# A weight conversion on four engines without its VectorE maximum: the scale of an activation keeps the shifted-out bits at zero

## The chip, the cores and the metric

The kernel runs on one core of a Trainium2 chip. The metric is the device time of one execution in microseconds (us). The kernel before takes 1225.82 us, the median of 3 runs between 1224.88 and 1225.98. One further execution was recorded by the hardware profiler, and every duration and wait that is quoted below comes from that one.

## The reference

The reference is an attention with random features, followed by a mixer over tokens and channels. The four weight tensors U, V, w_ch1 and w_ch2 of the mixer arrive as 64-bit floats, since `np.sqrt` makes them so; everything else is float32.

```python
# attention: batch 8, heads 8, sequence 576, head_dim 64, features 128
proj = x @ w_phi
proj = proj - max(abs(proj), axis=-1)
phi(x) = concat([exp(proj), exp(-proj)], axis=-1)
kv = sum over s of phi(k)[s,f] * v[s,d];  z = sum over s of phi(k)[s,f]
attn = (phi(q) @ kv) / (phi(q) @ z + 1e-6)
# mixer: x = attn as [8, 576, 512], U 576x32, V 32x576, w_ch1 512x2048, w_ch2 2048x512
u = x + (x^T @ U @ V)^T
out = u + max(u @ w_ch1, 0) @ w_ch2
```

## The kernel before

TensorE (PE) does all matrix products. A float32 operand that needs its full precision is split into a high and a low part, and three products (high by high, high by low, low by high) are summed. The hidden layer of the mixer is cut into 16 blocks f of 128 columns: `hidden` (line 619) makes one block of 512 tokens, and `add` (line 640) brings it through the second weight into the four output banks. One mixer pass g handles 512 tokens; there are nine of them. The attention of pairs of heads (`Pair`) runs in between, in steps such as `s_project_k0`, `s_kv1` or `s_out0`, and the class `Pace` hands out chunks of the mixer between the steps so that PE always has something to do.

The weights are loaded once, as 64-bit words, and converted on the chip. That is the function `convert` (line 130), called once for U, twice for V and 32 times for the blocks of w_ch1 and w_ch2 (two for each f). Each 64-bit float is turned into float32 like this. ScalarE (ACT) makes three pieces with three activations: two 16-bit pieces of the lower part (lines 137 and 138), and the size of the upper word, which is the absolute value of that word read as a float32, scaled by a power of two (line 140). VectorE (DVE) brings that size to a least value (line 141) and shifts its bits left by three (line 142), so that the 11-bit exponent of the 64-bit format becomes the 8-bit exponent of float32. GpSimd (POOL) adds the two halves as 64-bit integers (line 146). `split_w` then makes the two parts of the weight: a copy on ACT for w_ch1 or on DVE for w_ch2 (line 235), and a subtraction on DVE (line 236). In the names, `words` is the raw block, `w_ab` the scratch tile of the conversion, `w` the finished parts.

Only the first mixer pass (g = 0) needs blocks just converted; the conversions are spread over the time in which that pass and the attention of the first batches run (the constant `CONVERT`, and `blocks` in `mix`). On top of that, a scheduler sets the order of the instructions on each engine: it lays the whole program out with its own estimates of how long each instruction takes, so that leaving out one instruction can move others. Each engine then works through its list strictly in order. DVE, ACT and POOL are shared with the attention: line 348 and 350 (the maximum and the subtraction of the key features, `kp`), 364 (the subtraction of the query features, `qp`), 363 (the maximum over partitions on POOL for the query features), 625 (the low part of a hidden block, `h_lo`) and 319 (the low part of turned inputs, `T`) are the ones that matter below. PSUM banks are handed on in turn within a group: three banks carry the tag `at`, so a new tile there has to wait until the last reader of the tile that held its bank is done.

Of the kernel before, what the change touches and what calls it, by code (L numbers as in the profile page):

```python
# [16 lines left out]
AF = mybir.ActivationFunctionType  # L17
# [8 lines left out]
def tile_kernel(  # L26
# [12 lines left out]
    nc = tc.nc  # L39
# [33 lines left out]
    def f32(ap):  # L73
        return ap.bitcast(F32)
# [47 lines left out]
    def scratch(name, dt=F32, shape=(2, 512)):  # L122
        return moe.tile([P, *shape], dt, tag="wide", bufs=NW, name=name)
# [6 lines left out]
    def convert(st, name):  # L130

        n = st.shape[1]
        halves = st.rearrange("p n w -> p (n w)").bitcast(U16).rearrange("p (n h) -> p n h", h=4)
        ab = scratch(f"{name}_ab", I32)
        a, b_ = ab[:, 0, 0:n], ab[:, 1, 0:n]
        bh = b_.bitcast(U16).rearrange("p (n h) -> p n h", h=2)
        nc.scalar.activation(out=bh[:, :, 0], in_=halves[:, :, 1], func=AF.Copy, scale=2.0 ** -13)
        nc.scalar.activation(
            out=bh.bitcast(F16)[:, :, 1], in_=f32(st[:, :, 1]), func=AF.Copy, scale=2.0 ** -60)
        nc.scalar.activation(out=f32(a), in_=f32(st[:, :, 1]), func=AF.Abs, scale=2.0 ** -48)  # L140
        nc.vector.tensor_scalar_max(out=f32(a), in0=f32(a), scalar1=2.0 ** -63)
        nc.vector.tensor_scalar(  # L142
            out=a, in0=a, scalar1=3, scalar2=None, op0=ALU.logical_shift_left)

        a64, b64 = a.bitcast(U64), b_.bitcast(U64)
        nc.gpsimd.int64_add(a64, a64, b64)  # L146
        return f32(a)
# [3 lines left out]
    def load_uv():  # L151
        st = scratch("u_st", I32, (512, 2))[:, 0:(NT + 1) * R, :]
        sv = st.rearrange("p (t r) w -> p t r w", r=R)
        nc.sync.dma_start(
            out=sv[:, 0:NT], in_=U[0:SM].rearrange("(t p) r w -> p t r w", t=NT))
        for g in range(2):
            nc.sync.dma_start(out=sv[g * ST:(g + 1) * ST, NT], in_=U[SM:S])
        u_f = convert(st, "u").rearrange("p (t r) -> p t r", r=R)
        nc.vector.memset(f32(u_all[:, NT:NT + 2]), 0.0)
        parts = [(slice(0, P), slice(0, NT), slice(0, NT))]  # L160
        for g in range(2):
            parts.append((slice(g * ST, (g + 1) * ST), slice(NT + g, NT + g + 1), slice(NT, NT + 1)))
        for pr, to, of in parts:
            nc.vector.tensor_copy(out=u_all[pr, to, 0, :], in_=u_f[pr, of])
            nc.vector.tensor_sub(u_all[pr, to, 1, :], u_f[pr, of], f32(u_all[pr, to, 0, :]))
            for i in (2, 3):
                nc.vector.tensor_copy(out=u_all[pr, to, i, :], in_=f32(u_all[pr, to, 0, :]))

        for cs in (slice(0, SM), slice(SM, S)):
            n = cs.stop - cs.start  # L170
            st = scratch(f"v_st{cs.start}", I32, (512, 2))[:, 0:n, :]
            for g in range(4):
                nc.sync.dma_start(out=st[g * R:(g + 1) * R], in_=V[:, cs])
            v_f = convert(st, f"v{cs.start}")
            vm = v_all[:, cs]
            nc.vector.tensor_copy(out=vm, in_=v_f)
            lo = slice(3 * R, 4 * R)
            nc.vector.tensor_sub(vm[lo], v_f[lo], f32(vm[lo]))
# [36 lines left out]
    def convert_block(i):  # L215
        f, n = divmod(i, 2)
        r = convert(words[f][n], f"w{n + 1}_{f}")
        if f not in WHOLE:
            w = home.tile([P, 2, C], F32R, tag=f"w{n + 1}_{f}", name=f"w{n + 1}_{f}")
            split_w((nc.scalar.copy, nc.vector.tensor_copy)[n], r, w)  # L220
        elif n == 0:
            found[f] = r
            return
        else:
            w1_w, w = place(f, F32R, (2, C), f"w_{f}")
            split_w(nc.scalar.copy, found[f], w1_w)
            split_w(nc.vector.tensor_copy, r, w)
            w1_t[f] = w1_w
        (w1_t, w2_t)[n][f] = w
        if f in STREAM:  # L230
            for i in range(2) if f in WHOLE else (n,):
                nc.sync.dma_start(out=kept[f][:, i], in_=f32((w1_t, w2_t)[i][f]))
# [700 lines left out]
```

## Time and profile before

| what | value |
|---|---|
| median of 3 runs | 1225.82 us (1224.88 to 1225.98) |
| the profiled execution's own time | 1229.95 us |
| its span, first to last instruction | 1228.2 us |
| mean TensorE clock granted | 0.993 |
| busy: PE, DVE, ACT, POOL | 98%, 56%, 44%, 17% |
| line 141 on `w_ab` | 32 instructions, 20.3 us, 635 ns on average |
| first and last start of line 141 on `w_ab` | 47.3 us and 231.8 us |

A busy share is an average over the whole span. In the page's row of 40 slices a slice is about 31 us, and each digit is the busy share of that slice in tenths. "PEclk" is the clock that TensorE was granted, and 1.00 is full speed. The chain of waits goes back from the last instruction, at each step to what released it; a row of it gives the start, the time that this piece takes on the chain, the engine and the line. In a row of a group, the two figures behind the bar are the total busy time and the mean in ns of one instruction; consecutive instructions on DVE overlap a little, so a piece of the chain is shorter than the duration of its instruction.

### The profile page before, as it was taken

To read this page: it belongs to the slowest core of one execution; us is meant where nothing else is said; L and a number is where in the kernel's file an instruction comes from. 1 tells how busy PE (TensorE), PEld (TensorE's weight loads), DVE (VectorE), ACT (ScalarE), POOL (GpSimd) and SP (SyncE) were. 2 spreads that over 40 slices of the span, in tenths; PEclk is the share of its full clock that TensorE was granted. 3 is DMA by queue.
4 is the path that set the end of the run, shared out by engine and by line. 5 is a ranking of instruction groups with operands and counts; after the bars stand their busy time and mean duration, and the time that the engine had idled before them with its cause. 6 is when DMAs were issued, how large, how long until landed. Compare 5 with 4: busy or idle time off the path is not lost.

```text
span 1228.2 us, 18295 instructions
## 1 busy us (share of the span) xinstructions
PE 1204.1 (98%) x6667; PEld 1036.8 (84%) x6669; DVE 690.3 (56%) x1517; ACT 538.6 (44%) x1151; POOL 204.3 (17%) x154
## 2 busy tenths in 40 slices
PE   8999998999999999999999999999999999999998
PEld 7887887888888888888888888888888888888886
DVE  5858779775566656665556556755556543311211
ACT  6866678544443444444434444344534431111110
POOL 3533434211110111011111111011101110000000
PEclk9979999999999999999999999999999999999999
DMA  4766221341234213431244123431353014510201
GB/s 128 244 224 203 82 65 30 78 120 22 54 92 115 58 27 88 106 99 30 64 109 114 30 52 84 106 79 23 79 121 99 1 50 122 142 34 1 69 1 35
DMA packets 248409, 100.60 MB, mean 82 GB/s; under 512 B 215424, under 2 KB 227968, under 8 KB 248320
## 3 DMA queue, kind: packets, MB, share of 16 engines
q1 hardware_dynamic: 248000, 98.92, 31.0%
q8 instruction: 53, 0.87, 0.3%
q10 hardware_dynamic: 320, 0.52, 0.1%
q14 instruction: 36, 0.29, 0.1%
HBM read 78.41 MB, written 20.97 MB: 81 GB/s over the span
## 4 chain that ended last, share of the span: by engine, by line
PE 79%; DVE 7%; SPq 4%; ACT 4%; DMA 3%; issue 2%; POOL 0%; DVEq 0%; ACTq 0%; POOLq 0%
PE ph L619 27%; PE o L640 27%; PE xp L482 7%; PE kv_ps L443 7%; SPq L605 2%; PE pk L399 2%; DVE w L236 2%; SPq L265 1%; PE pp L561 1%; PE pq L422 1%; PE kv_ps L436 1%; PE pq L423 1%; DMA raw<-in_q_dram 1%; PE xpt L469 1%; DMA words<-in_moe_w_ch_dram 1%
## 5 line engine op out<-in xcount | busy, mean ns | idle before, releaser
L619 PE MATMUL ph<-uT_hi,w 128*128 128x512 f32 x1152 | 388.8, 395 | 4.2 <-DVE h_lo L625 2.9
L640 PE MATMUL o<-w,h_hi 128*128 128x512 f32 x1152 | 327.5, 395 | 3.0 <-ACT h_hi L624 3.0
L619 PEld LDWEIGHTS ph<-uT_hi,w 128*128 128x128 f32 x1152 | 216.2, 188 | 50.1 <-DVE h_lo L625 4.3
L640 PEld LDWEIGHTS o<-w,h_hi 128*128 128x128 f32 x1152 | 211.1, 188 | 45.1 <-ACT h_hi L624 4.7
L619 PE MATMUL ph<-uT_lo,w 128*128 128x512 f32 x576 | 225.1, 391 | 0.0
L624 ACT ACTIVATE h_hi<-ph 128x512 fp32r<-128x512 f32 x144 | 86.0, 597 | 268.2 <-PE ph L619 257.3
L625 DVE SCALAR_TENSOR_TENSOR h_lo<-ph,h_hi 128x512 fp32r<-128x512 f32 x144 | 98.6, 685 | 175.8 <-ACT h_hi L624 174.5
L640 PE MATMUL o<-w,h_lo 128*128 128x512 f32 x576 | 192.5, 395 | 0.4 <-DVE h_lo L625 0.4
L363 POOL PARTITION_ALL_REDUCE qp<-qp x64 | 127.3, 1989 | 288.2 <-ACT qp L362 269.7
L443 PEld LDWEIGHTS kv_ps<-vb,kp 128*128 128x128 f32 x1024 | 126.7, 195 | 2.8
L482 PEld LDWEIGHTS xp<-kv,qp 128*128 128x128 f32 x1024 | 124.0, 194 | 5.0 <-DVE kp L403 0.9
L619 PEld LDWEIGHTS ph<-uT_lo,w 128*128 128x128 f32 x576 | 108.3, 188 | 21.4 <-DVE uT_lo L244 0.6
L443 PE MATMUL kv_ps<-vb,kp 128*128 128x65 f32 x1024 | 126.1, 274 | 0.1
L482 PE MATMUL xp<-kv,qp 128*128 128x65 f32 x1024 | 124.1, 274 | 0.6 <-DVE kp L403 0.6
L640 PEld LDWEIGHTS o<-w,h_lo 128*128 128x128 f32 x576 | 105.4, 188 | 21.3 <-DVE h_lo L625 1.0
L353 ACT ACTIVATE kp<-kp 128x512 f32<-128x512 f32 x64 | 40.4, 631 | 134.4 <-DVE kp L350 79.4
L363 POOL PARTITION_ALL_REDUCE qp_t<-qp_t x32 | 27.3, 853 | 400.4 <-ACT qp_t L362 398.2
L319 DVE TENSOR_TENSOR T<-raw,T 64x512 fp32r<-64x512 f32 x96 | 67.6, 704 | 33.5 <-ACT T L318 31.0
L315 DVE STREAM_TRANSPOSE raw<-raw 128x512 f32<-128x512 f32 x48 | 34.1, 711 | 83.3 <-DMA raw<-in_q_dram 36.9
L318 ACT CAST T<-raw 64x512 fp32r<-64x512 f32 x96 | 59.3, 618 | 33.7 <-PE pq L423 18.2
L365 ACT ACTIVATE qp<-qp 128x512 f32<-128x512 f32 x64 | 40.4, 631 | 61.5 <-DVE qp L364 61.0
L146 POOL INT64_ADD w_ab<-w_ab x32 | 44.2, 1380 | 76.0 <-DVE w_ab L142 35.8
(128 smaller groups left out, 1357.7 us busy)
## 6 DMA issues: line engine op xcount, KB each, us to landing
words<-in_moe_w_ch_dram SPq DMA_DIRECT2D x32, 512.0 KB, 8.8
w<-kept SPq DMA_DIRECT2D x30, 512.0 KB, 4.0
vb<-in_v_dram SPq DMA_DIRECT2D x64, 128.0 KB, 2.5
u_dram<-x SPq DMA_DIRECT2D x32, 256.0 KB, 2.2
st<-u_dram SPq DMA_DIRECT2D x16, 512.0 KB, 3.9
out_dram<-st SPq DMA_DIRECT2D x32, 256.0 KB, 2.4
y<-u_dram SPq DMA_DIRECT2D x112, 64.0 KB, 2.4
raw<-in_k_dram SPq DMA_DIRECT2D x192, 32.0 KB, 2.0
```

Source lines behind the costliest of these rows:

```text
L146: nc.gpsimd.int64_add(a64, a64, b64)
L318: nc.scalar.copy(out=m[here, s, :], in_=x_[here])
L319: nc.vector.tensor_sub(m[there, s, :], x_[here], f32(m[here, s, :]))
L353: nc.scalar.activation(out=kp[:, :, 0:F], in_=kp[:, :, F:2 * F], func=AF.Exp)
L363: nc.gpsimd.partition_all_reduce(qp[:, 0, :], qp[:, 1, :], P, ReduceOp.absmax)
L365: nc.scalar.activation(out=qp[:, 0, :], in_=qp[:, 1, :], func=AF.Exp)
L443: nc.tensor.matmul(self.kv_v[:, f, g, :], kp[:, t, f * F:(f + 1) * F], self.vb[:, g, t, :], start=False, stop=(t == NT - 1), skip_group_ch ...
L482: nc.tensor.matmul(xv[:, c, :], qp[:, f, c * P:(c + 1) * P], self.kv[:, f, c // 2 if self.split else s, :], start=(f == 0), stop=(f == 1))
L619: nc.tensor.matmul(ph, w1_part(f, l, c), r[:, c, :], start=(n == 0), stop=(n == 3 * NCC - 1))
L624: on_act = nc.scalar.activation(out=h_hi, in_=ph, func=AF.Relu)
L625: on_dve = nc.vector.scalar_tensor_tensor(out=h_lo, in0=ph, scalar=0.0, in1=f32(h_hi), op0=ALU.max, op1=ALU.subtract)
L640: ins = nc.tensor.matmul(self.o[t], l[:, cs], w2_t[f][:, r, :], start=(f == 0 and n == 0), stop=(f == NFC - 1 and n == 2))
```

## The change

`convert` loses the maximum of line 141. The scale of the activation ahead of it goes from 2^-48 to 2^-112. Before, the scaled size still had the bit at the top of its exponent that the shift pushed out, and the maximum with 2^-63 made sure that this bit was always set. Now the exponent is so small that the bits which the shift pushes out are all zero. Below that, the shift and the integer addition are the same.

```diff
@@ convert
         nc.scalar.activation(
             out=bh.bitcast(F16)[:, :, 1], in_=f32(st[:, :, 1]), func=AF.Copy, scale=2.0 ** -60)
-        nc.scalar.activation(out=f32(a), in_=f32(st[:, :, 1]), func=AF.Abs, scale=2.0 ** -48)
-        nc.vector.tensor_scalar_max(out=f32(a), in0=f32(a), scalar1=2.0 ** -63)
+        nc.scalar.activation(out=f32(a), in_=f32(st[:, :, 1]), func=AF.Abs, scale=2.0 ** -112)
         nc.vector.tensor_scalar(
             out=a, in0=a, scalar1=3, scalar2=None, op0=ALU.logical_shift_left)
```

35 instructions leave DVE's list (32 of `w_ab`, two of V, one of U); no engine gets another one. The list of every engine is the same from about 270 us on; ahead of that, the scheduler has moved instructions. In the changed kernel the line numbers from 141 on are one lower: 141 is the shift there, 145 the integer addition, 234 and 235 the copy and the subtraction of a weight.

The first place is on DVE at about 54 to 60 us. `w_0` and `w_1` are the first two weight blocks (two conversions each), `pk_0_3` is the bank of projected keys that the last row frees. Before:

```order
L141 TENSOR_SCALAR w_1_ab<-w_1_ab 128x512
L461 TENSOR_TENSOR xt_267<-xpt_2_714,den_2_t_717 64x64
L456 TENSOR_SCALAR den_2_t_721<-xpt_2_714 64x1
L565 TENSOR_TENSOR pst_600<-pp_0_601,pst_600 32x256
L235 CAST w_0_928<-w_0_ab 128x512
L142 TENSOR_SCALAR w_1_ab<-w_1_ab 128x512
L141 TENSOR_SCALAR w_1_ab<-w_1_ab 128x512
L457 RECIPROCAL den_2_t_721<-den_2_t_721 64x1
L236 TENSOR_TENSOR w_0_891<-w_0_ab,w_0_891 128x512
L456 TENSOR_SCALAR den_2_0_734<-xp_0_2_725 128x4
L350 TENSOR_TENSOR kp_3_1_743<-pk_0_3_740,mk_3_1_744 128x4x128
```

And in the changed kernel:

```order
L347 TENSOR_REDUCE mk_3_1_741<-pk_0_3_737 128x4
L234 CAST w_0_923<-w_0_ab 128x512
L235 TENSOR_TENSOR w_0_887<-w_0_ab,w_0_887 128x512
L460 TENSOR_TENSOR xt_267<-xpt_2_711,den_2_t_714 64x64
L455 TENSOR_SCALAR den_2_t_718<-xpt_2_711 64x1
L141 TENSOR_SCALAR w_1_ab<-w_1_ab 128x512
L235 TENSOR_TENSOR w_0_923<-w_0_ab,w_0_923 128x512
L456 RECIPROCAL den_2_t_718<-den_2_t_718 64x1
L363 TENSOR_TENSOR qp_3_t<-qp_3_t 128x128
L455 TENSOR_SCALAR den_2_0_731<-xp_0_2_722 128x4
L349 TENSOR_TENSOR kp_3_1_740<-pk_0_3_737,mk_3_1_741 128x4x128
```

The second subtraction of `w_0`, the second shift of `w_1` and the subtraction of `qp_3_t` now stand ahead of the row that reads `pk_0_3` last; before, they came behind it.

The second place is on POOL at the same time (`ISA` on `w_ab` is the integer addition, on `qp` the maximum over partitions). Before:

```order
L146 ISA w_0_ab<-w_0_ab 128x512
L363 ISA qp_2_1_652<-qp_2_1_652 128x512
L309 MEMSET tail_T_0_787 128x256
L146 ISA w_0_ab<-w_0_ab 128x512
L363 ISA qp_3_t<-qp_3_t 128x128
L146 ISA w_1_ab<-w_1_ab 128x512 x2
```

And in the changed kernel:

```order
L145 ISA w_0_ab<-w_0_ab 128x512
L362 ISA qp_2_1_649<-qp_2_1_649 128x512
L145 ISA w_0_ab<-w_0_ab 128x512
L308 MEMSET tail_T_0_784 128x256
L145 ISA w_1_ab<-w_1_ab 128x512
L362 ISA qp_3_t<-qp_3_t 128x128
L145 ISA w_1_ab<-w_1_ab 128x512
```

The first addition of `w_1` now stands ahead of the maximum of `qp_3_t`.

The third place is on DVE at about 197 to 204 us, ahead of `h_lo_10`, the low part of a hidden block, for which PE waits. Before:

```order
L141 TENSOR_SCALAR w_13_ab<-w_13_ab 128x512
L297 TENSOR_TENSOR tail_T_0_2052<-tT_0_2050,tail_T_0_2052 64x2x64
L315 STREAM_TRANSPOSE raw_1_0_2160<-raw_1_0_2160 128x512
L142 TENSOR_SCALAR w_13_ab<-w_13_ab 128x512
L297 TENSOR_TENSOR tail_T_0_2052<-tT_0_2050,tail_T_0_2052 64x2x64
L319 TENSOR_TENSOR T_2_0_2063<-raw_0_1_1856,T_2_0_2063 64x512
L364 TENSOR_TENSOR qp_3_0_2017<-qp_3_0_2017 128x512
L319 TENSOR_TENSOR T_2_0_2063<-raw_0_1_1856,T_2_0_2063 64x512
L625 SCALAR_TENSOR_TENSOR h_lo_10_2135<-ph_10_2121,h_hi_10_2134 128x512
```

And in the changed kernel:

```order
L314 STREAM_TRANSPOSE raw_1_0_2130<-raw_1_0_2130 128x512
L141 TENSOR_SCALAR w_13_ab<-w_13_ab 128x512
L363 TENSOR_TENSOR qp_3_0_1990<-qp_3_0_1990 128x512
L296 TENSOR_TENSOR tail_T_0_2024<-tT_0_2022,tail_T_0_2024 64x2x64
L234 CAST w_12_2047<-w_12_ab 128x512
L318 TENSOR_TENSOR T_2_0_2035<-raw_0_1_1832,T_2_0_2035 64x512 x2
L235 TENSOR_TENSOR w_12_2047<-w_12_ab,w_12_2047 128x512
L296 TENSOR_TENSOR tail_T_0_2024<-tT_0_2022,tail_T_0_2024 64x2x64
L235 TENSOR_TENSOR w_13_2088<-w_13_ab,w_13_2088 128x512
L624 SCALAR_TENSOR_TENSOR h_lo_10_2105<-ph_10_2091,h_hi_10_2104 128x512
```

The first subtraction of `w_13` now stands ahead of `h_lo_10`; before, it came eight instructions behind it. (The copy and the subtraction of `w_12` came just ahead of the rows shown before.)

## The prediction

> **What bounds the kernel now.** I read the page first, then the stretches of time, then the chain of waits inside the stretch that counts.
>
> ```profile
> span 1228.2 us, 18295 instructions
> ...
> PE   8999998999999999999999999999999999999998
> PEld 7887887888888888888888888888888888888886
> DVE  5858779775566656665556556755556543311211
> ```
>
> PE is full nearly everywhere, and DVE is heavily loaded only in the first eight slices, up to about 250 us. The line that goes, 141, runs only there (47 to 232 us). Three stretches show what that means:
>
> ```profile
> 50.00:80.00 30.00, 28.37 (x155) 25.07 (x154) 21.11 (x53) 18.17 (x41) 11.90 (x10) 0.77 0.86 283
> 80.00:260.00 180.00, 168.14 (x956) 142.50 (x955) 145.28 (x288) 123.92 (x246) 64.09 (x44) 0.99 0.33 97
> 260.00:1228.00 968.00, 961.40 (x5255) 828.91 (x5254) 492.86 (x1088) 362.05 (x788) 109.21 (x69) 1.00 0.28 69
> ```
>
> The columns are the stretch, then busy time (and count) of PE, PEld, DVE, ACT and POOL, the granted clock, the DMA share and GB/s. From 260 us on PE is busy for 961.40 of 968 us with the same list in both kernels, so that part is 968 us whatever this change does. From 80 to 260 us PE is idle for 12 us, while DVE is busy for 145 of 180 us (81%), and the chain of waits in that stretch runs mostly over other engines than PE, whose largest part is 5.4%:
>
> ```profile
> by line: DVE w L236 9.5%; SPq L265 7.6%; issue 7.4%; PE o L640 5.4%; ACT w_ab L138 5.1%; PE ph L619 4.9%; ACT w_ab L137 4.9%; ACT w_ab L140 4.3%; DVE w L235 3.3%; PE xp L482 3.1%; DVE qp L364 3.1%; DVE T L319 2.9%; DMA raw<-in_q_dram 2.9%;
> ```
>
> So the question is how much earlier PE comes to the list it had at 260 us.
>
> **What goes.** The conversion's instructions:
>
> ```profile
> L137 ACT ACTIVATE w_ab<-words x32: 761/788/818, 45.3 to 229.8; 128x512 uint16<-128x512 uint16 x32
> L138 ACT ACTIVATE w_ab<-words x32: 745/769/799, 46.0 to 230.5; 128x512 f16<-128x512 f32 x32
> L140 ACT ACTIVATE w_ab<-words x32: 632/655/683, 46.6 to 231.1; 128x512 f32<-128x512 f32 x32
> L141 DVE TENSOR_SCALAR w_ab<-w_ab x32: 405/428/1544, 47.3 to 231.8; 128x512 f32<-128x512 f32 x32
> L142 DVE TENSOR_SCALAR w_ab<-w_ab x32: 384/427/1028, 47.8 to 232.2; 128x512 int32<-128x512 int32 x32
> L146 POOL INT64_ADD w_ab<-w_ab x32: 1266/1299/1740, 48.4 to 232.9; - x32
> L236 DVE TENSOR_TENSOR w<-w_ab,w x32: 643/688/1809, 57.0 to 236.2; 128x512 fp32r<-128x512 f32 x32
> ```
>
> (Least, median and longest duration in ns.) All 32 of line 141 together are busy for 20.3 us, but DVE is not the bound at every moment, so that total is not the gain. What counts is where line 141 stands on the chain of waits. Read in pieces from 40 to 260 us, the chain holds 13 of them, 4.85 us in all. The first, a long one, and the last four, which lie in a stretch where DVE has no idle time:
>
> ```profile
> 56.22 0.56 DVE w_ab L141
> ...
> 111.40 0.84 DVE w_ab L141
> ...
> 204.54 0.34 DVE w_ab L141
> ...
> 205.33 0.34 DVE w_ab L141
> ...
> 214.44 0.34 DVE w_ab L141
> ...
> 216.08 0.93 DVE w_ab L141
> ```
>
> An undisturbed one takes 0.34 us of the chain; the long ones (0.56, 0.84, 0.93) are stretched. The same stretching is seen on the neighbour at the first place:
>
> ```profile
> 55.97 1.03 POOL L363 PARTITION_ALL_REDUCE qp_t<-qp_t  x1 [2.18 <-DMA words<-in_moe_w_ch_dram]
> 56.91 1.34 POOL L146 INT64_ADD w_ab<-w_ab  x1
> ```
> ```profile
> 56.98 1.81 DVE w L236
> ...
> 58.99 0.61 DVE kp L350
> ```
>
> Line 236, 0.69 us as a rule, starts just after the addition on POOL and ends 0.54 us after it: DVE waited for POOL. A stretched line 141 is such a wait too, and if it is gone, its successor (the shift, which runs at the same speed on the same tile) waits instead. So I count each piece with at most 0.34 us: the 13 pieces then come to 3.53 us instead of 4.85. The one of U, before the first of these, adds 0.24 us (its duration; it is also on the chain).
>
> The Trainium skill ("SBUF — State Buffer", section "Who interferes with whom") states this as a rule: DVE in a mode with two ports, or with two SBUF inputs, and GpSimd share a port pair under an exclusive lock, and the later one is fully blocked until the first has finished. By that rule the stretch is inherited and the pieces are worth 3.53 us; without it the whole 4.85 us would be. The rows above agree with the rule (a start 0.07 us after POOL's, an end after POOL's end).
>
> **What moves.** At the first place PE waited:
>
> ```profile
> 59.64 0.38 PE L436 MATMUL kv_ps<-vt,kp_t 128*128 128x130 f32 x1 [1.39 <-DVE kp L350]
> ```
>
> `kv_ps` gets the bank of `pk_0_3`, whose last reader is that `kp` row of line 350. From the copy of `kv_2` to this row DVE has 22 instructions in both kernels: three of line 141 have gone, and the second shift of `w_1` (0.34), the second subtraction of `w_0` (0.60 on the chain) and the subtraction of `qp_3_t` (0.21) have come ahead. That is 1.15 us for 3 x 0.34 = 1.02 or, with the stretch of 0.56, 1.24 us: nothing won there. The added POOL wait, of `qp_3_t` behind an addition of `w_1` moved ahead of its maximum, need not cost: the addition (1.30 us) fits into the 2.18 us in which POOL was idle before that maximum, and only if its shift is late does it push. So the 0.34 us of the first place fall away. Behind `kp`, PE's products for `kv` are queued, and behind these the steps of the next pair.
>
> At the third place PE waited for `h_lo_10`:
>
> ```profile
> 204.26 0.50 PE L619 MATMUL ph<-uT_hi,w 128*128 128x512 f32 x1 [1.60 <-DVE h_lo L625]
> ```
>
> The change takes one line 141 away ahead of it (0.34) and brings one subtraction of `w_13` (0.60): a loss of 0.26 us here, and 1.3 us more if the subtraction has to wait for its own addition on POOL. All of PE's `hidden` is queued behind it. What is moved behind `h_lo_10` is freed later, so this is a shift of work, not new work.
>
> The other edits cost nothing: the activation of line 140 is the same instruction with another constant (0.655 us), and the shift loses only its wait for line 141. DMA issues move by a place or two on SP. The cover for all that is PE's own load, and without it each would cost its 0.4 to 0.7 us.
>
> **Sum.** 3.53 + 0.24 - 0.34 - 0.26 = 3.2 us gained. The profiled execution took 1229.95 us, so the changed one would take 1226.8 there. The median of the runs lies 4.1 us below the profiled execution, and I take the same gain from it: 1222.6 us. Bounds: at most all of the chain, 4.85 + 0.24 = 5.1 us (1220.7); at least only the four pieces at 204 to 217 us, where DVE has no slack, 4 x 0.34 less the 0.26, 1.1 us (1224.7).
>
> **The rivals.** The clock is one. Where PE had waited at the first place, the clock fell soon after:
>
> ```profile
> 62.00:74.00 12.00, 12.00 (x48) 10.91 (x49) 4.27 (x12) 3.82 (x9) 3.99 (x2) 0.50 1.03 352
> 92.00:94.00 2.00, 2.00 (x5) 1.21 (x5) 1.97 (x4) 0.00 (x0) 1.19 (x1) 0.50 1.03 349
> 200.00:210.00 10.00, 7.51 (x35) 5.68 (x33) 9.87 (x14) 7.95 (x16) 5.84 (x4) 1.00 0.23 41
> ```
>
> From 62 to 74 us half the clock is granted, with PE full and alone on the chain; 12 us at 0.50 cost 6 us, the edges some 0.8 more. *Rival 1: this stretch goes*, because the gap of 1.39 us gets a little shorter. That gives 3.2 + 6.8 = 10.0 us, 1215.8 us. For it: any shorter gap may do. Against it: the order at the first place wins nothing, as worked out above.
>
> The Trainium skill ("TensorE: Matmul & The Clock Gate", Part 1) has the clock fall to half after an idle window of about 3.4 us. By that alone neither gap would cost any clock, and rival 1 could win nothing by a shorter one. The trace differs: 1.39 us were enough at 59 us, while 1.60 us at 204 us were not.
>
> *Rival 2, slower: a second such stretch comes.* The place is PE's gap ahead of `h_lo_10`, 1.60 us with the clock still at 1.00, and the change brings a subtraction in front of it. If the gap grows by the 0.26 to 1.3 us above and the clock falls as at 62 us, that costs 6.8 us against the 3.2 gained: 1229.4 us. It decides from the point where the clock falls for about 12 us; a gap alone, even 1.3 us longer, would leave the kernel faster. For it: DVE is at 9.87 of 10 us there. Against it: four lines 141 near it go.
>
> *Rival 3, no change: ACT takes the bound.* The three activations take 2.2 us for each conversion, 71 us in all, and of DVE's own waits in 50 to 250 us the longest is
>
> ```profile
> DVE w_ab L141 <- ACT w_ab L140: 9.2, 14, 1.5
> ```
>
> so in 14 of 32 cases DVE stood ready and ACT was late. If the saved 0.34 us only lengthen that wait, the gain is 0 to 1.1 us: 1225.3 us. For it: those 14 waits. Against it: when ACT is late, the shift still comes 0.34 us sooner behind it, and so do the addition and the subtraction.
>
> That the change might not do what it says I give no chance: one DVE instruction fewer for each conversion stands in the lists.
>
> **How the numbers follow.** Forecast 0.52, rival 1 0.17, rival 2 0.12, rival 3 0.19. About 0.2% (2.5 us) is what a measurement of this kernel can tell from no change, so faster means under 1223.4 us. Of the forecast's own range, 1220.7 to 1224.7, about two thirds lie under that: 0.35. Faster: 0.35 + 0.17 = 0.52; within 0.2%: 0.17 + 0.19 = 0.36; slower: 0.12. The range takes in rival 1 and rival 3, with a little on each side for shifted lists, and leaves out rival 2: 1214.5 to 1228.5.
>
> **What would show it.** Right: no row of 128x512 float32 maximum, the point where the list of 260 us begins comes 1 to 5 us earlier, and the stretch from 260 us on is as long as before. The chain between 80 and 260 us holds the shift behind line 140's activation, and no longer pieces of the shift than 0.34 us but for those that inherit a wait for POOL. Wrong: the granted clock at 60 to 76 us is 1.00 (rival 1); it is 0.50 somewhere around 205 us (rival 2); DVE's wait for ACT's size activation grows by as much as line 141 took (rival 3); or the list after 260 us takes another time than before, against all I assume.

## The result: 1219.14 us, 6.7 us less

The changed kernel takes 1219.14 us (median of 5 runs, 1218.24 to 1221.31) where the kernel before, run beside it, takes 1225.82 (5 runs, 1224.53 to 1229.54). The ratio is 0.9946, with a 95% interval from 0.9927 to 0.9966. Forecast were 1222.6 us and a gain of 3.2 us, with 5.1 us as the upper bound of the sum: the sign and the wide range held, but the size came to less than half of the 6.7 us, and the forecast's own range (1220.7 to 1224.7) is missed by 1.6 us. Its profiled execution took 1218.74 us, with a mean clock of 0.997 where that of before had 0.993.

The page of the changed kernel, the lines that answer to those of before:

```profile
span 1216.9 us, 18254 instructions
...
PE   8999998999999999999999999999999999999998
PEld 7878887888888888888888888888888888888886
DVE  5866777765556556755556656665656542311211
```

PE is full as before, and DVE still loaded up to about 250 us, with lower digits in three of the six slices from 92 to 276 us. The stretches of time, cut where the list stands that the kernel before reached at 260 us (the columns are those of the prediction):

```profile
50.00:80.00 30.00, 26.41 (x183) 22.36 (x182) 22.86 (x57) 23.07 (x53) 12.67 (x11) 1.00 0.86 282
80.00:247.30 167.30, 160.39 (x923) 139.05 (x924) 121.06 (x250) 118.26 (x232) 61.65 (x43) 0.99 0.35 102
247.30:1216.90 969.60, 962.22 (x5255) 829.13 (x5254) 493.96 (x1088) 361.84 (x788) 108.89 (x69) 1.00 0.28 69
```

The list reached at 260.0 us before is reached at 247.3 now, 12.7 us earlier. What follows it takes 969.6 us instead of 968.2, with the same 5255 matmuls. In the first stretch the granted clock is 1.00, where it was 0.77. Of the 12.7 us, 6.85 are clock: before, the clock was at 0.50 for 17.1 us (13.7 from 60.9 us, 3.4 from 91.6 us), now for 3.4 us (from 193.3 us), and a difference of 13.7 us at half speed is 6.85 us of work. The other 5.9 us are work and waits, and the stretch behind takes 1.4 us of them back, so that over the whole span this one pair differs by 4.4 us beside the clock, which lies within the sum's bounds; over many executions it is more (6.8 us, below). So before anything else is compared, the clock has to be set aside: over the 35 executions of the kernel before that ran beside the first experiments, the time falls by 1.1 us for each 0.001 of mean clock. Where a time is called **at equal clock** below, each execution is brought to 0.997 with 1 us per 0.001, and the figure is the mean with 1.96 standard errors on either side (for a kernel with only six executions a 95% interval is about a third wider). The mean clock is a rough measure: in 11 of the 14 profiled executions it also fell behind the last matmul, where that costs nothing, by as much as 1.5 us of lost clock. So differences at equal clock of less than about 1 us are not read below. One execution in all that follows, of the kernel called "before, other spread", took 1321.15 us at a mean clock of 0.851 and is left out of that kernel's figures.

The chain of waits in the stretch between 80 us and the list of 260, in the changed kernel:

```profile
by line: PE ph L618 18.4%; PE o L639 17.0%; issue 6.0%; PE xp L481 5.6%; PE kv_ps L442 4.2%; DVE T L318 3.6%; DVE w L235 3.5%; SPq L264 3.5%; POOL w_ab L145 2.5%; ACT w_ab L138 2.5%; DVE uT_lo L243 2.2%; DVE x L577 2.1%; DVE w L234 1.9%; AC
```

Before, this line began with the subtraction of a weight (9.5%), and PE's largest part was 5.4%. Now PE's two mixer products alone hold 35%: the stretch was bound by the conversions and what shares their engines, and is now bound by PE for about half of it.

### The profile page after: what moved, and what is told of

The parts are those of the page before. It is cut to its first block, busy times and chain, and to the rows that moved or that the text cites. A ratio compares the mean times of both kernels' runs of the same rounds, so it can differ in the third digit from the quotient of the medians.

```text
span 1216.9 us, 18254 instructions
## 1 busy us (share of the span) xinstructions
PE 1195.1 (98%) x6669; PEld 1031.3 (85%) x6669; DVE 668.7 (55%) x1482; ACT 538.9 (44%) x1151; POOL 204.5 (17%) x154
## 4 chain that ended last, share of the span: by engine, by line
PE 80%; DVE 7%; SPq 5%; DMA 3%; ACT 3%; issue 2%; POOL 0%; DVEq 0%; ACTq 0%; POOLq 0%
PE ph L618 28%; PE o L639 28%; PE xp L481 7%; PE kv_ps L442 7%; SPq L604 3%; PE pp L560 2%; PE pk L398 1%; SPq L264 1%; PE kv_ps L435 1%; PE pq L421 1%; DMA u_dram<-x 1%; DMA y<-u_dram 1%; PE xpt L468 1%; PE pq L422 1%; DVE T L318 1%
## 5 line engine op out<-in xcount | busy, mean ns | idle before, releaser
L442 PEld LDWEIGHTS kv_ps<-vb,kp 128*128 128x128 f32 x1024 | 124.0, 192 | 2.8
L442 PE MATMUL kv_ps<-vb,kp 128*128 128x65 f32 x1024 | 123.5, 270 | 0.0
L317 ACT CAST T<-raw 64x512 fp32r<-64x512 f32 x96 | 59.3, 618 | 33.5 <-PE pq L422 20.6
```

The costliest lines, as they stand in the source:

```text
L317: nc.scalar.copy(out=m[here, s, :], in_=x_[here])
L442: nc.tensor.matmul(self.kv_v[:, f, g, :], kp[:, t, f * F:(f + 1) * F], self.vb[:, g, t, :], start=False, stop=(t == NT - 1), skip_group_ch ...
```

## The experiments

"The change again", "before, size first" and so on name the kernels below. Each ran 6 or 12 times beside the kernel before; the first four share one set of executions of it (35), and the next four and the last four another each (17). "Stretch" is worked out from the trace of the one profiled execution: for each DVE instruction between 45 and 262 us, what it lasts beyond the shortest of its own form, counted where that is over 0.15 us. The last column is the part of it that lies on the DVE instructions writing `w_ab` (maximum, shift, or both in one).

| kernel | median, us | ratio (95%) | at equal clock, us | DVE stretch, us | on `w_ab`, us |
|---|---|---|---|---|---|
| before | 1227.64 | 1 | 1226.5 ± 0.4 | 26.5 | 7.9 |
| the change again | 1218.93 | 0.9935 (0.9912 to 0.9958) | 1219.7 ± 0.6 | 15.4 | 0.4 |
| two maxima | 1232.57 | 1.0042 (1.0020 to 1.0065) | 1229.4 ± 0.7 | 29.4 | 10.4 |
| before, size first | 1224.71 | 0.9977 (0.9959 to 0.9995) | 1223.3 ± 0.5 | 26.7 | 12.2 |
| change, size first | 1225.92 | 0.9988 (0.9966 to 1.0010) | 1225.1 ± 0.7 | 26.4 | 9.0 |
| narrow maximum | 1220.45 | 0.9938 (0.9913 to 0.9962) | 1220.5 ± 1.3 | 23.3 | 5.8 |
| change in blocks 0 to 7 | 1219.76 | 0.9932 (0.9907 to 0.9956) | 1221.9 ± 1.3 | 20.6 | 4.4 |
| change in blocks 8 to 15 | 1227.43 | 0.9982 (0.9963 to 1.0002) | 1223.1 ± 0.8 | 19.4 | 3.8 |
| change, shift and or | 1214.77 | 0.9890 (0.9866 to 0.9914) | 1215.8 ± 0.4 | 5.6 | 0 |
| before, shift and or | 1215.66 | 0.9880 (0.9854 to 0.9905) | 1216.5 ± 1.1 | 8.3 | 2.1 |
| change, shift and or, again | 1215.59 | 0.9885 (0.9866 to 0.9906) | 1216.2 ± 0.7 | 5.5 | 0 |
| before, other spread | 1228.01 | 0.9999 (0.9982 to 1.0016) | 1225.8 ± 0.9 | 23.1 | 9.0 |
| change, other spread | 1216.04 | 0.9906 (0.9878 to 0.9935) | 1218.8 ± 0.7 | 15.9 | 3.6 |

The kernel before had medians of 1229.65 and 1227.50 beside the second and third group, and at equal clock 1226.2 and 1226.4. In every kernel, each stretched DVE instruction ran while POOL was at work.

### The change again, and two maxima

The first is the change itself, the second the kernel before with line 141 twice:

```diff
         nc.vector.tensor_scalar_max(out=f32(a), in0=f32(a), scalar1=2.0 ** -63)
+        nc.vector.tensor_scalar_max(out=f32(a), in0=f32(a), scalar1=2.0 ** -63)
```

> The changed kernel once more, beside the kernel before on the same chip, with the granted clock of each run. All theories: 5 to 8 us faster than before. Theory 'clock' (part of the 6.7 us is that the changed kernel meets no long half-clock stretch): the runs of the kernel before that lie high have a lower mean clock, and runs of equal clock differ by only about 3 us. Theory 'DVE time' (the gain is DVE's time alone): at equal clock they still differ by 6 to 7 us.

> The kernel before with the maximum done twice in each conversion (the second changes nothing). Theory 'chain' (each maximum costs what it takes on the chain, 3.2 to 5.1 us for all): 1229 to 1231 us, 3 to 5 us above before. Theory 'DVE time' (each costs about 0.2 us of end time, as the 6.7 us of the change say): 1231 to 1234 us. Theory 'order' (the scheduler's new lists made the gain, the maximum's own time matters little): anywhere within 5 us of before, on either side.

At equal clock the change gains 6.8 us, twice the forecast, as the theory 'DVE time' had it; the theory 'clock' falls. A second maximum, though, costs only 2.9 us (4.9 in medians, the rest of which is clock: a mean of 0.993 where the kernel before had 0.995). So the maximum has no fixed price per instruction: the same instruction is worth 6.8 us when it goes and 2.9 when it comes again.

### The size's activation first

In the kernel before and in the changed one, the activation of line 140 is moved ahead of those of lines 137 and 138, so that the maximum and the shift can run while ACT makes the other two pieces:

```diff
+        nc.scalar.activation(out=f32(a), in_=f32(st[:, :, 1]), func=AF.Abs, scale=2.0 ** -48)
         nc.scalar.activation(out=bh[:, :, 0], in_=halves[:, :, 1], func=AF.Copy, scale=2.0 ** -13)
...
-        nc.scalar.activation(out=f32(a), in_=f32(st[:, :, 1]), func=AF.Abs, scale=2.0 ** -48)
```

> The kernel before with the size activation (line 140) put ahead of the other two, so that the maximum and the shift can run on DVE while ACT still makes the other two pieces (1.4 us). Theory 'chain' (the maximum counts as latency between ACT and POOL): most of the gain comes by this too, 1220 to 1223 us, and it differs from the changed kernel with the same edit by less than 1.5 us. Theory 'DVE time' (it counts as occupancy of DVE): 1224 to 1226 us, and still 5 to 7 us above the changed kernel with the same edit.

> The changed kernel with the size activation put ahead of the other two, so that the shift too runs beside ACT. Theory 'chain': 1216 to 1219 us, and within 1.5 us of the kernel before with the same edit. Theory 'DVE time': 1217 to 1220 us, 5 to 7 us below the kernel before with the same edit.

In this order the change gains nothing; at equal clock it is 1.8 us the slower of the two. Both theories had put it at 1216 to 1220 us, and both were wrong. The rows of `w_ab` on DVE (least, median, longest in ns), with the maximum:

```profile
L141 DVE TENSOR_SCALAR w_ab<-w_ab x32: 385/424/1491, 45.8 to 224.8; 128x512 f32<-128x512 f32 x32
L142 DVE TENSOR_SCALAR w_ab<-w_ab x32: 398/426/1423, 46.2 to 225.3; 128x512 int32<-128x512 int32 x32
```

and without it:

```profile
L141 DVE TENSOR_SCALAR w_ab<-w_ab x32: 399/427/1210, 44.5 to 225.0; 128x512 int32<-128x512 int32 x32
```

Here the shift without the maximum is still stretched, to 1210 ns at the longest, and 9.0 of the 12.2 us of stretch on `w_ab` stay. That is what the prediction had assumed of the change: the successor inherits the wait. Where it does, the gain is indeed gone. But these two kernels' lists differ from the others in many more places (the scheduler moves instructions on every engine, on DVE up to about 400 us), so that this pair alone can't show that the stretch is the reason.

### A narrow maximum, and half of the change

The narrow one keeps an instruction in line 141's place, on 2 of the 512 columns; the other two leave the maximum out for one half of the weight blocks (the diff shows the first half; for the second it is f >= 8):

```diff
-        nc.vector.tensor_scalar_max(out=f32(a), in0=f32(a), scalar1=2.0 ** -63)
+        nc.vector.tensor_scalar_max(out=f32(a[:, 0:2]), in0=f32(a[:, 0:2]), scalar1=0.0)
```
```diff
+        if not bare:
             nc.vector.tensor_scalar_max(out=f32(a), in0=f32(a), scalar1=2.0 ** -63)
...
+        r = convert(words[f][n], f"w{n + 1}_{f}", f < 8)
```

> The changed kernel, with a maximum put back that works on 2 of the 512 columns only (with zero, so it changes nothing): 35 instructions more in DVE's list, and the wait between ACT and the shift goes through them, but almost no DVE time. The first four runs gave, at an equal clock of 0.997, about 1219.7 us with no maximum, 1226.5 with one and 1229.4 with two. Theory 'DVE time' (about 3 us for each maximum by its duration): 1219 to 1222 us at that clock. Theory 'order' (the list of the kernel before is an unlucky one, worth the other 3 us, or that of the changed kernel a lucky one): the list here is a third one, so anything from 1219 to 1227 us.

> The maximum is left out only in the conversions of the blocks f below 8 (U, V and the blocks from 8 on keep it and the old scale). Theory 'DVE time': half of the gain or a little less, 1222 to 1224 us at a clock of 0.997. Theory 'first wait' (the gain of the early stretch, where PE's gap at 59 us and the half clock lie): most of the gain, 1219 to 1221 us. Theory 'order': no rule, and the two halves do not add up to the whole.

> The maximum is left out only in the conversions of the blocks f from 8 on. Theory 'DVE time', with the four pieces at 204 to 217 us of the forecast: half of the gain or a little more, 1222 to 1224 us at a clock of 0.997. Theory 'first wait': 1225 to 1227 us. Theory 'order': the two halves do not add up to the 6.8 us of the whole.

With the narrow maximum 5.7 ± 1.5 of the 6.8 us are still gained at equal clock (1226.2 - 1220.5): one more instruction in DVE's list, with its handing over, costs little; what costs is its length, be it as time of DVE or as delay of what follows, which this run does not separate. The halves gain 4.3 ± 1.5 and 3.1 ± 1.1 us, together about the whole. In medians they gain 9.9 and 2.2 us, which looks like the theory 'first wait'; the difference is clock, with means of 0.999 and 0.994. So the gain at equal clock is not made in one place, such as the 204 to 217 us that carried the prediction's lower bound.

### No addition on POOL: shift and or

A DVE instruction that shifts and then takes the bitwise or with the lower part replaces the shift on DVE and the addition on POOL; the lowest three bits are prepared with another scale so that they do not overlap:

```diff
-        nc.vector.tensor_scalar(
-            out=a, in0=a, scalar1=3, scalar2=None, op0=ALU.logical_shift_left)
-        a64, b64 = a.bitcast(U64), b_.bitcast(U64)
-        nc.gpsimd.int64_add(a64, a64, b64)
+        nc.vector.scalar_tensor_tensor(
+            out=a, in0=a, scalar=3, in1=b_, op0=ALU.logical_shift_left, op1=ALU.bitwise_or)
```

> A version that may beat both: the shift and the joining of the two halves are one DVE instruction (shift left by three, then bitwise or, 128x512 with two SBUF inputs, about 0.69 us), and GpSimd's 64-bit addition (1.30 us, 35 times) goes. For that the three low bits are scaled so that they round to at most 7 and never carry, which changes the last bit of some converted weights. Theory 'DVE time': DVE gets 0.26 us more for each conversion, 32 x 0.26 = 8 us of which a quarter lies on the chain (2 us), and loses the waits for POOL's lock (the stretched 1.4 to 1.8 us instructions) and the 1.3 us of latency: 1214 to 1219 us. Theory 'order': within 5 us of 1222 on either side.

> The kernel before, its maximum kept, but with the shift and the joining of the two halves in one DVE instruction (a shift and a bitwise or) in place of the shift on DVE and the 64-bit addition on POOL; the lowest three bits are prepared with another scale for that. The same without the maximum took 1214.8 us. Theory A (waits for POOL: what the change gains beyond 3.2 us are waits behind the additions that hung on the maximum): with no addition there is nothing to wait behind, the maximum costs only its own place, and this kernel takes about 1217 to 1218.5 us, 2 to 4 us above the one without. Theory B (DVE's time: about a third of the maximum's 20 us are felt, whoever stands beside): 1221 to 1222, 6 to 7 us above. Theory C (slack: the conversion is shorter by 1.3 us, so that the maximum hides): within 1 us of 1214.8.

> The kernel of the shift and the bitwise or without the maximum again, beside the one with it, so that both are compared on the same chip. All theories: 1214 to 1216 us, as before.

This is the sharpest of the experiments. With the addition on POOL the maximum costs 6.8 us; without it 0.3 ± 1.3 us. The time is that of theory C; theory B falls, and theory A's 2 to 4 us are too much (2 us only just, if the wider interval of six executions is taken). The kernel with the maximum, in which `w_ab` is written on DVE:

```profile
L141 DVE TENSOR_SCALAR w_ab<-w_ab x32: 385/427/543, 45.5 to 216.3; 128x512 f32<-128x512 f32 x32
L142 DVE SCALAR_TENSOR_TENSOR w_ab<-w_ab x32: 664/692/1659, 46.0 to 217.2; 128x512 int32<-128x512 int32 x32
```

The maximum has the same median as before (427 ns), but its longest is 543 ns instead of 1544. And DVE was not idle: between 80 and 240 us, the kernel before, this one with the maximum and the one without it (PE, PEld, DVE, ACT, POOL busy and so on):

```profile
80.00:240.00 160.00, 150.14 (x851) 127.33 (x851) 131.06 (x256) 116.14 (x229) 64.09 (x44) 0.99 0.32 94
```
```profile
80.00:240.00 160.00, 154.97 (x867) 132.83 (x867) 128.50 (x265) 113.05 (x222) 23.35 (x15) 0.99 0.35 104
```
```profile
80.00:240.00 160.00, 156.61 (x882) 134.39 (x882) 120.16 (x245) 113.91 (x225) 22.63 (x15) 0.99 0.36 106
```

DVE is busy for 128.5 us with the maximum, nearly as long as before the change (131.1), and PE gets through 155 us of work instead of 150. So DVE's load as such is not what the maximum's price hangs on. What differs is the addition on POOL (busy for 64 us there and for 23 here), and with it both the waits for POOL and the 1.30 us that the addition adds to each conversion. The chain of waits in this stretch, with the maximum and without it:

```profile
by line: PE ph L616 21.8%; PE o L637 17.2%; PE xp L479 6.5%; SPq L262 4.4%; PE kv_ps L440 4.3%; DVE T L316 3.7%; PE pq L424 3.4%; PE pk L381 3.3%; DMA raw<-in_q_dram 2.4%; issue 2.2%; DVE uT_lo L241 1.6%; DVE st L658 1.5%; DVE w L233 1.3%; 
```
```profile
by line: PE ph L615 30.2%; PE o L636 27.5%; PE xp L478 8.9%; PE kv_ps L439 8.6%; PE pq L423 4.0%; PE pk L380 3.3%; DMA words<-in_moe_w_ch_dram 2.4%; PE vp L573 1.6%; DVE st L657 1.5%; PE pt L589 1.5%; PE pp L557 1.5%; DVE uT_lo L240 1.4%; P
```

Without POOL's addition PE's products lead the chain in both, and the conversions (`w_ab`) are not among the rows shown: the maximum hides. All three runs of this form (1214.77 to 1215.66 us) beat the changed kernel (1218.93), by 3.3 to 4.2 us.

### Another spread of the conversions

In both kernels the conversions are spread over the steps 24 to 62 instead of 24 to 63:

```diff
-    CONVERT = (24, 63)
+    CONVERT = (24, 62)
```

> The kernel before with its conversions spread over the steps 24 to 62 in place of 24 to 63, which gives the planner another order for what comes between 100 and 250 us, and no other work. It is the base for the next run. Theory D (the size of the gain is a matter of the one order that the planner found): this kernel may lie anywhere from 1220 to 1232. Theories A and B: 1224 to 1228, since the work is the same.

> The change, with its conversions spread over the steps 24 to 62. Theories A and B: 5.5 to 7.5 us below the run of the kernel before with the same spread. Theory D: the difference is another one, 0 to 4 us or 9 and more.

In medians the gain is 12.0 us, which looks like theory D. At equal clock it is 7.0 ± 1.1 us, as theories A and B had it: the rest is clock, at a mean of 0.994 with the maximum and 0.998 without it. So the gain of some 7 us is not a matter of one single order. That it can be lost altogether, the pair with the size first shows.

## Why the prediction was right, and where it was short

**PE full from 260 us on: held, but for 1.4 us.** The last of the three stretches is that much longer, though the prediction had taken it to be the same. In the last 3.1 us of the span the clock was low, but no engine was at work there any more, so that is not the reason:

```profile
1213.80:1216.90 3.10, 0.00 (x0) 0.00 (x0) 0.00 (x0) 0.00 (x0) 0.00 (x0) 0.51 0.41 136
```

Matmul by matmul, the lead over the kernel before falls from 12.7 us where the list of 260 us begins to 11.2 us at the last matmul, at full clock and in steps of 0.5 us or less (the two largest at about 386 and 922 us of the kernel before). What makes them is not shown.

**The first place: the order held, the wait did not get shorter.** The chain ahead of `kp` in the changed kernel, and PE's wait behind it:

```profile
56.42 0.43 DVE w_ab L141
56.85 0.61 DVE w L235
...
57.67 1.05 DVE qp_t L363
...
58.92 0.61 DVE kp L349
```
```profile
59.57 0.71 PE L435 MATMUL kv_ps<-vt,kp_t 128*128 128x130 f32 x4 [1.65 <-DVE kp L349]
```

PE starts at 59.57 us instead of 59.64, and has waited 1.65 us instead of 1.39: nothing won, as worked out. The added wait for POOL, on `qp_3_t`, was there too: that subtraction takes 1.05 us of the chain.

**The third place: a wait moved.** PE no longer waits for `h_lo_10`; it waits a little earlier, until 192.7 us, for the low part of a tail, behind a run of DVE instructions without a gap, among them the copy and the subtraction of `w_12` that the change brought there (start, piece of the chain, both in us; then the longest wait of the stretch):

```profile
188.09 1.10 DVE w L234
...
189.22 1.54 DVE T L318
...
190.79 0.70 DVE T L318
...
191.51 0.69 DVE w L235
...
192.23 0.31 DVE tail_T L296
...
192.67 0.30 PE pkt L372
```
```profile
PE pkt L372 <- DVE tail_T L296: 3.1, 1, 3.1
```

From the hidden block 8 to the block 10 the lead over the kernel before falls from 10.4 to 9.9 us (the start of the `h_hi` activation of each), a loss of 0.5 us where 0.26 was forecast.

**The step that failed: "if it is gone, its successor waits instead".** Each piece of line 141 on the chain was counted with at most 0.34 us, since its stretch would be inherited by the shift, and line 236 was not counted at all. That gave 3.2 us; the gain at equal clock is 6.8 ± 0.7. The tile in the changed kernel:

```profile
L140 ACT ACTIVATE w_ab<-words x32: 626/650/692, 45.5 to 220.4; 128x512 f32<-128x512 f32 x32
L141 DVE TENSOR_SCALAR w_ab<-w_ab x32: 384/427/641, 46.1 to 221.1; 128x512 int32<-128x512 int32 x32
L145 POOL INT64_ADD w_ab<-w_ab x32: 1276/1296/1822, 46.8 to 221.7; - x32
L235 DVE TENSOR_TENSOR w<-w_ab,w x32: 660/689/1772, 55.2 to 226.8; 128x512 fp32r<-128x512 f32 x32
```

The shift, line 141 now, has 641 ns at the longest: it inherited next to nothing, though POOL's additions are as many and as long as ever (32, 1296 ns), and line 235 still has a longest of 1772. The activation of line 140 with its other constant takes 650 ns, as before (655).

Where the wait went can be read from the times of two conversions in a row. Before (start, duration, both in us):

```profile
110.65 1.31 POOL L146 INT64_ADD w_ab<-w_ab  x1 [3.46 <-DVE w_ab L142]
```
```profile
111.40 0.83 DVE L141 TENSOR_SCALAR w_ab<-w_ab 128x512 f32<-128x512 f32 x1 [0.94 <-ACT w_ab L140]
```

and in the changed kernel:

```profile
101.30 1.30 POOL L145 INT64_ADD w_ab<-w_ab  x1 [2.46 <-DVE w_ab L141]
```
```profile
102.97 0.42 DVE L141 TENSOR_SCALAR w_ab<-w_ab 128x512 int32<-128x512 int32 x1
```

In both, the addition is that of one conversion and the DVE row is the first of the next, whose activation of line 140 starts 1.8 us after that of the one before. With the maximum, the addition ends at 111.96 us, when the next size has been ready since 111.37; without it, it ends at 102.60, when the next size has just come (102.54). Before, nine of the 32 maxima ran into an addition like this and took over 0.8 us, and each ended behind it, eight of them by 0.27 to 0.29 us. In the change only one shift did, by a little (641 ns). With the size first, the next size comes earlier than the last piece that the addition waits for, and there eleven of the 32 shifts without a maximum ran into an addition: that is why the wait stayed in that kernel. So the maximum, by putting the addition some 0.46 us later, helped to make the meetings that stretched it. For four of the nine (stretched by 0.4 to 0.5 us) that delay is long enough; for the other five (0.6 to 1.1 us) other delays on DVE had a part, and how large a part is not shown.

On the whole, DVE's stretch fell from 26.5 to 15.4 us, and not on `w_ab` alone (7.9 to 0.6) but on the subtractions of the weights (8.6 to 6.3), on copies (4.3 to 2.7) and, by 0.6 us, on the features of the queries; on the low parts `T` it rose (1.1 to 2.7). The same piece of the program, from hidden block 10 to the first of the next pass, before and after:

```profile
200.10:259.00 58.90, 53.38 (x299) 44.79 (x298) 51.13 (x101) 34.03 (x71) 14.54 (x10) 1.00 0.28 78
```
```profile
190.10:246.30 56.20, 52.97 (x294) 45.69 (x295) 45.88 (x97) 32.22 (x67) 13.30 (x9) 0.97 0.29 82
```

There it takes 58.9 us before and 56.2 after, 1.7 of which are half clock: 4.4 us less at equal clock. DVE is busy for 51.1 us before and for 45.9 after. Five of the maxima stand there, 2.6 us; the other 2.6 us and more are stretches of other lines that are gone (6.5 us before, 2.8 after). The prediction's lower bound came from this place, 1.1 us; in this pair of executions it was the place of most of the gain, though the early half of the change alone gains 4.3 us as well. Even the upper bound, 5.1 us for all pieces of line 141 on the chain, left out what the others lost.

What the runs show is that the price of the maximum depends on the additions on POOL (6.8 us with, 0.3 without), and that the gain went along with a stretch that disappeared where it was gained (7.9 to 0.6, 9.0 to 3.6) and stayed where nothing was (12.2 to 9.0). That the waits for POOL are the cause of the extra 3.6 us, and not the shorter way from ACT over DVE and POOL to the finished weight, is argued from this and not shown: the kernels without the addition take away both. Against the stretch as the only cause speak the narrow maximum (23.3 us of stretch and still a gain) and the size first (26.4 us with the change, like 26.5 before, but 1.4 us faster than that). What remains open, too, is why a second maximum costs 2.9 us and not 6.8.

The Trainium skill ("SBUF — State Buffer", section "Who interferes with whom") has only the later of two instructions wait for the lock, for as long as the other runs. The long maxima agree with it (1544 ns with the additions, 543 without). But to work out that the successor inherits the wait, as the prediction did, is no part of that rule: whether the next instruction finds an addition running depends on when both start, as the rows above show.

**Rival 1, the clock: the stretch went, but not by a shorter wait.** The granted clock in the stretch that the prediction showed, and where PE waited at the third place:

```profile
62.00:74.00 12.00, 12.00 (x91) 11.24 (x90) 7.32 (x22) 7.32 (x16) 4.90 (x4) 1.00 1.00 351
190.00:200.00 10.00, 7.33 (x31) 6.13 (x31) 8.87 (x17) 7.42 (x16) 3.83 (x3) 0.83 0.22 39
```

The sign that the prediction had named for this rival came: the stretch of 62 to 74 us is at 1.00, though the wait ahead of it got longer and not shorter. In the kernel before with the other spread, the same wait at the same time is followed by a low clock of 3.4 us instead of 13.7:

```profile
59.63 0.71 PE L436 MATMUL kv_ps<-vt,kp_t 128*128 128x130 f32 x4 [1.41 <-DVE kp L350]
```
```profile
61.40:64.80 3.40, 3.40 (x15) 3.04 (x13) 2.59 (x5) 1.86 (x5) 1.82 (x2) 0.50 0.89 260
64.80:75.00 10.20, 10.20 (x77) 9.53 (x77) 7.22 (x22) 5.57 (x13) 4.02 (x4) 1.00 1.07 378
```

The two lists are the same up to there. So most of the 6.8 us that the prediction gave this stretch belonged to that execution and not to the list: of the 35 executions of the kernel before, 14 had a mean clock of 0.994 or less and the others more, and of the 12 of the change four had. That is why the profiled pair differs by more (11.3 us of span) than the medians (6.7). The rival's condition, a shorter wait, was wrong.

**Rival 2, a second stretch at half clock: it came, but short.** The wait of 3.1 us at the third place was followed by 3.4 us at 0.50, 0.83 in the row above, which costs 1.7 us and not 6.8. In the change with the other spread this wait is missing, and with it the low clock:

```profile
50.00:80.00 30.00, 26.40 (x184) 22.36 (x183) 22.79 (x57) 23.08 (x53) 12.79 (x11) 1.00 0.86 282
180.00:200.00 20.00, 19.05 (x114) 16.53 (x112) 15.82 (x29) 17.02 (x35) 10.78 (x7) 1.00 0.25 46
```

**Rival 3, ACT as the bound: no.** DVE's wait for the size's activation went from 9.2 to

```profile
DVE w_ab L141 <- ACT w_ab L140: 14.0, 14, 3.0
```

It is the same 14 times and 4.8 us longer, where line 141 had taken 20.3 us: part of the saved time went there, most of it did not.

## What to carry to other kernels

A piece of a chain that is longer than usual because it met another engine on a shared resource is not bound to be handed on: with the instruction gone, both engines' next ones start at other times, and may not meet. Lay the two engines' rows side by side and see whether the instruction itself made them meet; if so, count the stretch as gain in the upper bound, for the neighbours too. Before a gain of half a per cent is taken from two profiles, set the clock aside: compare executions at the same mean granted clock, or many of them. And when an instruction's price hangs on a neighbour engine, ask first whether that engine's step is needed at all: putting the addition into the shift was worth more than the maximum.

## What the runs showed of the hardware

The granted clock fell to 0.50 for multiples of 3.4 us (3.4, 6.8, 13.7), and for how long differed where the lists were the same. The two waits of PE of 1.39 and 1.41 us, at the same place, were followed by 13.7 and 3.4 us of it, while one of 1.65 us was followed by none. The Trainium skill ("TensorE: Matmul & The Clock Gate", Part 1) has the clock judged over free-running windows of about 3.4 us; the lengths agree with that, but the low clock came here behind waits of 1.4 us, far shorter than a window.

A DVE instruction that ran into a POOL addition ended 0.27 to 0.29 us behind it in nearly every case (eight of nine maxima before, all eleven shifts with the size first in the changed kernel).

A DVE shift and bitwise or of two 128x512 words takes 0.69 us, against 0.43 us for the shift and 1.30 us for the addition on POOL that it replaces.
